# Attention and two MLP layers: weight conversions bound to later steps, flips of two pairs in other banks, norms and splits in another order

## The chip, the cores and the metric

The kernel runs on one core of a Trainium2 chip. The time is device time of one execution in microseconds (us), the median of several runs; lower is better.

## What is computed

```python
q_n, k_n = rmsnorm(q, g_q), rmsnorm(k, g_k)          # q, k, v: 4 x 12 heads x 448 x 64, f32
attn = softmax(q_n @ k_n.T / sqrt(64))               # per head, over 448 keys
x = (attn @ v)                                       # laid out as 1792 tokens x 768
h = x @ w_in;  x = (s * relu(h)**2 + b) @ w_out      # 768 -> 2048 -> 768, weights 64 bit
h = x @ w2_in; out = (h * cos(h)) @ w2_out           # 768 -> 2048 -> 768, weights 64 bit
```

## The kernel before

**Attention.** There are 24 pairs of heads (4 batches of 448 tokens, 6 pairs each). Pairs are numbered here by their index from 0; a pair has four steps s = 4i to 4i + 3, one for each chunk of 112 queries. `attention` is a generator whose loop emits one step per turn: scores of both heads (two matmuls into `sc` banks), their row maxima on VectorE (`top`), the Exp on ScalarE (`pr`, which also gives the row sums), and for the step two back `turn`: transposes of `pr` on TensorE into `tp` banks, copied out as `pT` by ScalarE for one head and by VectorE for the other. In step 1 and 2 of a pair the next pair's normalised q and k are transposed by `flip` (`pt_q`, `pt_k`) and copied out by `unflip` (`qT` on ScalarE, `kT` on VectorE). In steps 2 and 3 `mix` multiplies the previous pair's `pT` by v (`av`), `spread` transposes the reciprocals of the row sums (`rt`, copied to `xf`), and in step 0 of the pair after it `finish` multiplies the two on VectorE. Norms go ahead by two or three pairs: `squares`, `means`, `norms`, on GpSimd for most pairs and on VectorE for pair 0. `scores` of a step waits for the Exp of two steps before it.

**Splits.** All matmuls of the two layers work in two parts, high and low, and three products. `split` (called by `keep` at the end of a pair of the first two batches) makes them of x: `xh` on ScalarE (L96), `xl` on GpSimd (L97). `load_weight` makes them of the weights, in blocks of 128 x 384: a raw 64-bit block is loaded (queue SP), ScalarE converts its high and low words (`c` L392, `t` L393), VectorE joins them in three steps (L397 `t`, L398 `c`, L399 `t`), the result is stored for later use (L402), and `halves` makes `wh` on ScalarE (L359) and `wl` on GpSimd (L360). Two blocks make one weight tile; tiles wh and wl have three buffers each. The first blocks in order: two tiles of w_in (blocks 1 to 4), two of w_out (5 to 8), two of w_in (9 to 12), and so on.

**Stages.** The first nine pairs run alone (`ALONE = 9`). From step 40 on, units of the first layer are emitted between the steps of the remaining pairs: `unit_in` (18 matmuls `ph`, L422) and `unit_out` (6 matmuls `po`, L474), at a rate worked out from costs. The first group is two ph tiles and six po sums of batch 0, the next begins with two further w_in tiles.

**Banks.** `bank` gives a pair with index under 9 the two banks `mo` of pool `psm` for flips, spread and sums, which from step 40 on are also those of `ph` and `po`; later pairs take the two `tp` banks, which the transposes of `turn` use too.

**Order.** A scheduler places the instructions of each engine's queue by a model of their times, and pulls an instruction forward where it thinks the engine idle, except where the program fixes an order: `line` chains the instructions it is given on one engine (on ScalarE and VectorE while no more than 36 Exps have been emitted), `issue_after` puts one instruction behind another in the queue of the same engine without a wait. c and t of the first 16 blocks are put behind an Exp of `exps`, the list of the second Exp of each step: block number p (from 0) behind step GATE + 4p for p up to 7, then two steps apart. With GATE = 8 that is the first step of pairs 2 to 9. wh, wl, xh and xl are bound to nothing.

Of the kernel before, what the change touches and what calls it, by code (L numbers as in the profile page):

```python
# [10 lines left out]
F32 = mybir.dt.float32  # L11
# [4 lines left out]
ALU = mybir.AluOpType  # L16
# [17 lines left out]
def body(ctx, tc, q, k, v, g_q, g_k, w1_in, w1_out, s_in, b_in, w2_in, w2_out, out):  # L34
    nc = tc.nc
# [3 lines left out]
    P = 128  # L39
# [9 lines left out]
    NT = 2 * S // P  # L49
    SKEW = 2  # L50
    LAG_T = 2
    START, GATE = 4, 8
    ALONE = 9
    PAIR = 12.1
    LOOK = 8
# [55 lines left out]
    def attention(keep):  # L111
        att, ps = pools["att"], pools["ps"]
        pairs = [(b, hp) for b in range(B) for hp in range(NP)]
        st = [dict() for _ in pairs]
        tail = {}

        def line(engine, first, last=None):
            if engine in tail and (engine == "PE" or len(exps) <= NCH * ALONE):
# [38 lines left out]
        def norms(i):  # L157
            b, hp = pairs[i]
            m, tiny = st[i]["m"], nc.vector if i == 0 else nc.gpsimd
            ln = att.tile([CP, 16], F32, tag="ln", name=f"ln_{b}_{hp}")  # L160
            line("ACT", nc.scalar.activation(ln, m, AF.Ln))
            y = att.tile([CP, 16], F32, tag="y", name=f"y_{b}_{hp}")
            line("ACT", nc.scalar.activation(y, ln, AF.Exp, scale=-0.5))
            z = att.tile([CP, 16], F32, tag="z", name=f"z_{b}_{hp}")
            tiny.tensor_tensor(z, y, y, ALU.mult)
            tiny.tensor_tensor(z, z, m, ALU.mult)
            tiny.tensor_scalar(z, z, -0.5, 1.5, ALU.mult, ALU.add)
            tiny.tensor_tensor(y, y, z, ALU.mult)
            rs = y.rearrange("p (a h c) -> p a h c", a=2, h=2)
            if i == 0:  # L170
                st[i]["rs"] = y[:, 0:2 * NCH]
            for n, nm in enumerate("qk"):
                if i == 0 and n == 0:
                    continue
                (nc.vector if i == 0 else nc.gpsimd).tensor_tensor(
                    st[i]["n" + nm].rearrange("p c h d -> p h c d"), st[i][nm],
                    rs[:, n].unsqueeze(3).to_broadcast([CP, 2, NCH, D]), ALU.mult)

        def bank(i, name):
            if i < ALONE:  # L180
                return psm.tile([P, 512], F32, tag="mo", name=name, bufs=2)
            return ps.tile([P, 512], F32, tag="tp", name=name)

        def flip(i, nm):
            b, hp = pairs[i]
            pt = bank(i, f"pt_{nm}_{b}_{hp}")[:, :S]
            src = st[i]["q by chunk"] if i == 0 and nm == "q" else st[i]["n" + nm]
            mm = [nc.tensor.transpose(pt[:, c * CP:(c + 1) * CP], src[:, c, :, :].rearrange("p h d -> p (h d)"), ident[:CP, :CP]) for c in range(NCH)]
            line("PE", mm[0], mm[-1])
            st[i]["p" + nm] = pt  # L190
# [63 lines left out]
        def spread(i):  # L254
            b, hp = pairs[i]
            rt = bank(i, f"rt_{b}_{hp}")[:, :S]
            mm = [nc.tensor.transpose(rt[:, c * CP:(c + 1) * CP], st[i]["rb"][:, c, :, :].rearrange("p h d -> p (h d)"), ident[:CP, :CP]) for c in range(NCH)]
            line("PE", mm[0], mm[-1])
            x = st[i]["x"] = att.tile([P, S], F32, tag="xf", name=f"xf_{b}_{hp}", bufs=1)
            line("ACT", nc.scalar.copy(x, rt))  # L260

        def mix(i, part):
# [11 lines left out]
        def finish(i):  # L274
            b, hp = pairs[i]
            x = st[i]["x"]
            line("DVE", nc.vector.tensor_tensor(x, st[i]["pa"], x, ALU.mult))
            keep(b, hp, x)
            st[i].clear()
            finished["pairs"] += 1  # L280

        def emit(f, i, *a):
            if 0 <= i < len(pairs):
# [19 lines left out]
        for s in range(n + 5):  # L303
            i, r = divmod(s, NCH)
            old = i - 1 if 0 < i <= len(pairs) else None
            alone = old is not None and old < ALONE
            cost = 0.0
            if r == 1:
                emit(load, i, "v")
                emit(flip, i + 1, "q")  # L310
                cost += 0.46
            if r == 2:
                emit(flip, i + 1, "k")
                cost += 0.46
            if s < n:
                scores(s)
                cost += 0.93
            if r == 1:
                emit(unflip, i + 1, "q")
            if r == 2:  # L320
                emit(unflip, i + 1, "k")
            if r == 3 and old is not None and not alone:
                finish(old)
            if LAG_T <= s < n + LAG_T:
                turn(s - LAG_T)
                cost += 0.9
            if r == 0:
                if 0 <= i - 2 < ALONE:
                    finish(i - 2)
                emit(reciprocals, i - 1)  # L330
            if r == 2 and old is not None:
                if alone:
                    mix(old, range(2))
                else:
                    spread(old)
                    mix(old, range(NCH))
                cost += 3.86
            if r == 3 and alone:
                spread(old)
                mix(old, range(2, NCH))  # L340
            if i == 0 and r in (1, 2):
                for part in ((squares,), (means, norms))[r - 1]:
                    part(2)
            if r == 0 and i > 0:
                emit(norms, i + 2)
            if r == 2:
                emit(squares, i + 3)
            if r == 3:
                emit(means, i + 3)
                emit(load, i + 4, "qk")  # L350
            yield cost
# [3 lines left out]
    plain = {}  # L355
    count = {"g": 0, "raw": 0}

    def halves(w, wh, wl, eng=nc.gpsimd):
        nc.scalar.copy(wh, w)  # L359
        eng.tensor_tensor(wl, w, wh.bitcast(F32), ALU.subtract)  # L360

    def load_weight(key):
        layer, seg, kind, a, e = key
        w = ((w1_in, w1_out), (w2_in, w2_out))[layer][kind]
        name = "_".join(map(str, key))
        wh = wp.tile([P, 2 * CW], F32R, tag="wh", name=f"wh_{name}", bufs=3)
        wl = wp.tile([P, 2 * CW], F32R, tag="wl", name=f"wl_{name}", bufs=3)
        weights[key] = wh, wl
        for o in range(2):
            kk = f"{name}_{o}"  # L370
            hi_part, lo_part = (z[:, o * CW:(o + 1) * CW] for z in (wh, wl))
            if (layer, kind, a, e, o) in plain:
                t = wp.tile([P, CW], F32, tag="t", name=f"t_{kk}", bufs=3)
                nc.sync.dma_start(t, plain[layer, kind, a, e, o])
                halves(t, hi_part, lo_part, nc.vector)
                continue
            own = "xb" in pools or count["raw"] % 3 < 2
            raw = (wp if own else pools["att"]).tile([P, CW], I64, tag="raw", name=f"raw_{kk}", bufs=2 if own else 1)
            count["raw"] += 1
            if kind == 0:  # L380
                src = w[o * CW:(o + 1) * CW, a * P:(a + 1) * P].rearrange("(c p) f -> p c f", p=P)
                dma = nc.sync.dma_start(raw.rearrange("p (c f) -> p c f", f=P), src)
            else:
                dma = nc.sync.dma_start(raw, w[(CF * a + o) * P:(CF * a + o + 1) * P, e * CW:(e + 1) * CW])
            if seg == 0 and kind == 0 and a == 0:
                follow(dma, marks["start"])
            ru = raw.bitcast(U32).rearrange("p (n two) -> p n two", two=2)
            lo, hi = ru[:, :, 0], ru[:, :, 1]
            c = wp.tile([P, CW], U32, tag="c", name=f"c_{kk}", bufs=2)
            cf = c.bitcast(F32)  # L390
            t = wp.tile([P, CW], U32, tag="t", name=f"t_{kk}", bufs=3)
            for z in (nc.scalar.activation(cf, hi.bitcast(F32), AF.Copy, scale=2.0**-112),  # L392
                      nc.scalar.activation(t, lo, AF.Copy, scale=LSCALE, bias=-0.5)):  # L393
                p = count["raw"] - 1
                if p < 16:
                    issue_after(z, exps[min(GATE + 4 * min(p, 7) + 2 * max(p - 7, 0), len(exps) - 1)])
            nc.vector.scalar_tensor_tensor(t, hi, 0x80000000, t, ALU.bitwise_and, ALU.bitwise_or)  # L397
            nc.vector.tensor_scalar(cf, cf, VMAX, -VMAX, ALU.min, ALU.max)  # L398
            nc.vector.scalar_tensor_tensor(t, c, 3, t, ALU.logical_shift_left, ALU.bitwise_or)  # L399
            if layer == 0:  # L400
                d = dram.tile([P, CW], F32, tag=f"w_{kk}", name=f"wd_{kk}")
                nc.sync.dma_start(d, t.bitcast(F32))  # L402
                plain[layer, kind, a, e, o] = d
            halves(t.bitcast(F32), hi_part, lo_part)


    g = {}
# [264 lines left out]
```

## Time and profile before

| | us |
|---|---|
| median of 3 runs | 1315.2 (1314.98 to 1315.31) |
| the profiled execution | 1311.66 |
| its span, first to last instruction | 1309.9 |
| TensorE busy | 1251.1 (96%) |
| VectorE busy | 850.3 (65%) |
| ScalarE busy | 745.4 (57%) |
| GpSimd busy | 585.5 (45%) |

In the rows PE is TensorE's matmuls, PEld its weight loads, DVE VectorE, ACT ScalarE, POOL GpSimd; L228 is a line of the kernel; `tp<-ident,pr` names what is written and read. Clocks are TensorE's granted clock, 1.00 for 2.4 GHz and 0.50 for 1.2 GHz. Matmul ends are modelled, so that a busy TensorE is not one at its peak.

### The profile page before, as it was taken

How to read it: one execution, taken by the hardware profiler on the slowest of the kernel's cores; microseconds unless marked ns; L12 is line 12 of the kernel's file. 1: busy time of each engine (PE TensorE's matmuls, PEld its weight loads, DVE VectorE, ACT ScalarE, POOL GpSimd, SP SyncE). 2: the span in 40 equal slices, each digit the busy share in tenths (PEclk: the TensorE clock that was granted, in tenths of full speed). 3: DMA queues.
4: the chain of work that ended last, by engine and by line, in shares of the span. 5: the costliest groups of instructions: out<-in, count | busy, mean ns of one | idle time of the engine just before them, and what ended most of it. 6: DMA issues, size and time to landing. Idle time of an engine off the chain costs nothing.

```text
span 1309.9 us, 18652 instructions
## 1 busy us (share of the span) xinstructions
PE 1251.1 (96%) x6624; PEld 1036.7 (79%) x6624; DVE 850.3 (65%) x1456; ACT 745.4 (57%) x1674; POOL 585.5 (45%) x643
## 2 busy tenths in 40 slices
PE   5988998999999999999999999999999999999998
PEld 3444575677676666779999999989999999999997
DVE  6787666867777675664344545864767767666655
ACT  5676666756665555534432334788656657565641
POOL 4666454644545434234332233554544445354531
PEclk9999999999999999999999999999999999999999
DMA  4333332543434233254221212121212221111105
GB/s 120 94 90 93 93 107 75 164 136 102 137 101 131 94 90 114 82 177 125 78 81 49 61 55 73 41 69 49 61 36 73 60 62 49 49 49 49 49 14 169
DMA packets 82222, 111.33 MB, mean 85 GB/s; under 512 B 8112, under 2 KB 72144, under 8 KB 82128
## 3 DMA queue, kind: packets, MB, share of 16 engines
q1 hardware_dynamic: 82128, 110.13, 28.3%
q8 instruction: 52, 0.85, 0.3%
q14 instruction: 42, 0.34, 0.1%
HBM read 86.51 MB, written 23.59 MB: 84 GB/s over the span
## 4 chain that ended last, share of the span: by engine, by line
PE 64%; DVE 12%; ACT 11%; DMA 5%; POOL 3%; issue 3%; SPq 0%; ACTq 0%; DVEq 0%; POOLq 0%
PE ph L422 25%; PE po L501 15%; PE po L474 13%; PE av L269 4%; PE sc L208 4%; ACT pr L228 3%; PE tp L246 3%; DVE t L397 3%; DMA raw<-in_moe_w_in_dram 3%; DVE top L220 2%; ACT c L392 1%; DVE t L399 1%; DVE gt L447 1%; ACT pT L252 1%; DMA raw<-in_moe_w_out_dram 1%
## 5 line engine op out<-in xcount | busy, mean ns | idle before, releaser
L422 PE MATMUL ph<-xh,wl 128*128 128x448 f32 x768 | 283.5, 369 | 0.0
L422 PE MATMUL ph<-xh,wh 128*128 128x448 f32 x768 | 281.0, 371 | 1.6 <-ACT hs L440 1.6
L422 PE MATMUL ph<-xl,wh 128*128 128x448 f32 x768 | 282.4, 368 | 0.0
L452 POOL TENSOR_TENSOR gl<-gt,gh 128x448 fp32r<-128x448 f32 x128 | 157.7, 1237 | 180.0 <-ACT gh L451 179.9
L360 POOL TENSOR_TENSOR wl<-t,wh 128x384 fp32r<-128x384 f32 x128 | 139.0, 1103 | 91.7 <-ACT wh L359 85.6
L228 ACT ACTIVATE pr<-sc,top 112x448 f32<-112x448 f32 x184 | 116.2, 636 | 78.8 <-DVE top L220 78.4
L422 PEld LDWEIGHTS ph<-xh,wh 128*128 128x128 f32 x768 | 144.6, 188 | 19.5 <-issue 2.7
L501 PE MATMUL po<-wh,gh 128*128 128x384 f32 x448 | 151.9, 339 | 3.6 <-DVE acc L509 1.7
L474 PE MATMUL po<-gh,wh 128*128 128x448 f32 x384 | 145.7, 381 | 9.7 <-DVE acc L483 9.1
L422 PEld LDWEIGHTS ph<-xl,wh 128*128 128x128 f32 x768 | 144.7, 188 | 11.7 <-issue 1.3
L422 PEld LDWEIGHTS ph<-xh,wl 128*128 128x128 f32 x768 | 144.8, 188 | 11.3 <-issue 1.3
L483 DVE TENSOR_TENSOR acc<-po,acc 128x448 f32<-128x448 f32 x168 | 103.0, 618 | 77.7 <-PE po L474 77.5
L501 PE MATMUL po<-wh,gl 128*128 128x384 f32 x448 | 149.8, 334 | 0.0
L359 ACT CAST wh<-t 128x384 fp32r<-128x384 f32 x200 | 95.2, 512 | 95.7 <-PE po L474 52.3
L501 PE MATMUL po<-wl,gh 128*128 128x384 f32 x448 | 149.5, 334 | 0.0
L474 PE MATMUL po<-gh,wl 128*128 128x448 f32 x384 | 141.7, 369 | 0.0
L474 PE MATMUL po<-gl,wh 128*128 128x448 f32 x384 | 141.4, 369 | 0.0
L220 DVE TENSOR_REDUCE top<-sc 112x1 f32<-112x448 f32 x192 | 112.8, 616 | 38.1 <-PE sc L208 37.8
L509 DVE TENSOR_TENSOR acc<-po,acc 128x384 f32<-128x384 f32 x196 | 105.2, 550 | 48.4 <-PE po L501 48.4
L246 PEld LDWEIGHTS tp<-ident,pr 112*112 112x112 f32 x768 | 79.3, 134 | 71.6 <-issue 19.8
L450 POOL TENSOR_TENSOR gt<-hs,gt 128x448 f32<-128x448 f32 x64 | 78.6, 1228 | 118.9 <-ACT gt L449 108.7
L392 ACT ACTIVATE c<-raw 128x384 f32<-128x384 f32 x128 | 70.9, 554 | 103.7 <-DMA raw<-in_moe_w_in_dram 41.9
(89 smaller groups left out, 2261.0 us busy)
## 6 DMA issues: line engine op xcount, KB each, us to landing
raw<-in_moe_w_in_dram SPq DMA_DIRECT2D x64, 384.0 KB, 3.5
raw<-in_moe_w_out_dram SPq DMA_DIRECT2D x64, 384.0 KB, 3.2
t<-wd SPq DMA_DIRECT2D x72, 192.0 KB, 2.4
wd<-t SPq DMA_DIRECT2D x64, 192.0 KB, 3.4
rawk<-in_k_dram SPq DMA_DIRECT2D x24, 224.0 KB, 3.1
rawv<-in_v_dram SPq DMA_DIRECT2D x24, 224.0 KB, 3.4
rawq<-in_q_dram SPq DMA_DIRECT2D x23, 224.0 KB, 2.6
xd<-xf SPq DMA_DIRECT2D x12, 224.0 KB, 3.7
```

What stands on the lines that cost most here:

```text
L220: line("DVE", nc.vector.tensor_reduce(tops[j], sc[j], axis=AX.X, op=ALU.max, negate=True))
L228: e = line("ACT", nc.scalar.activation(pr, sc[j], AF.Exp, bias=tops[j], scale=scale[j], accum_out=st[i]["sums"][:, c, j:j + 1]))
L246: mm = [nc.tensor.transpose(tp[:, kc * CP:(kc + 1) * CP], pr[:, kc * CP:(kc + 1) * CP], ident[:CP, :CP]) for kc in range(NCH)]
L359: nc.scalar.copy(wh, w)
L360: eng.tensor_tensor(wl, w, wh.bitcast(F32), ALU.subtract)
L392: for z in (nc.scalar.activation(cf, hi.bitcast(F32), AF.Copy, scale=2.0**-112), nc.scalar.activation(t, lo, AF.Copy, scale=LSCALE, bias=- ...
L422: nc.tensor.matmul(h, a, m, start=(c == 0 and n == 0), stop=(c == NE - 1 and n == 2))
L452: nc.gpsimd.tensor_tensor(gl, gt, gh.bitcast(F32), ALU.subtract)
L474: marks["out"] = nc.tensor.matmul(po, a, m, start=(f == 0 and n == 0), stop=(f == CF - 1 and n == 2))
L483: nc.vector.tensor_tensor(at, po, at, ALU.add)
L501: nc.tensor.matmul(po, a, m, start=(f == 0 and n == 0), stop=(f == CF - 1 and n == 2))
L509: nc.vector.tensor_tensor(at, po, at, ALU.add)
```

## The change

c and t of every gated block are bound two steps later: behind the third step's Exp of pairs 2 to 9 for the first eight blocks, and two steps later for the others too. wh of the first eight blocks is bound behind the Exp of the step after that. The flips of pairs 9 and 10 take the `mo` banks. The vector steps of pair 0's norms are chained on VectorE in program order. For pairs 0 to 7 `keep` (xh, xl) is emitted in the fourth step after `mix` instead of in the first step, and `xf` has two buffers for it.

```diff
@@ -49,7 +49,7 @@
     NT = 2 * S // P
     SKEW = 2
     LAG_T = 2
-    START, GATE = 4, 8
+    START, GATE = 4, 10
     ALONE = 9
     PAIR = 12.1
     LOOK = 8
@@ -113,6 +113,7 @@
         pairs = [(b, hp) for b in range(B) for hp in range(NP)]
         st = [dict() for _ in pairs]
         tail = {}
+        held = []
 
         def line(engine, first, last=None):
             if engine in tail and (engine == "PE" or len(exps) <= NCH * ALONE):
@@ -162,19 +163,20 @@
             y = att.tile([CP, 16], F32, tag="y", name=f"y_{b}_{hp}")
             line("ACT", nc.scalar.activation(y, ln, AF.Exp, scale=-0.5))
             z = att.tile([CP, 16], F32, tag="z", name=f"z_{b}_{hp}")
-            tiny.tensor_tensor(z, y, y, ALU.mult)
-            tiny.tensor_tensor(z, z, m, ALU.mult)
-            tiny.tensor_scalar(z, z, -0.5, 1.5, ALU.mult, ALU.add)
-            tiny.tensor_tensor(y, y, z, ALU.mult)
+            kept = (lambda z: line("DVE", z)) if i == 0 else lambda z: z
+            kept(tiny.tensor_tensor(z, y, y, ALU.mult))
+            kept(tiny.tensor_tensor(z, z, m, ALU.mult))
+            kept(tiny.tensor_scalar(z, z, -0.5, 1.5, ALU.mult, ALU.add))
+            kept(tiny.tensor_tensor(y, y, z, ALU.mult))
             rs = y.rearrange("p (a h c) -> p a h c", a=2, h=2)
             if i == 0:
                 st[i]["rs"] = y[:, 0:2 * NCH]
             for n, nm in enumerate("qk"):
                 if i == 0 and n == 0:
                     continue
-                (nc.vector if i == 0 else nc.gpsimd).tensor_tensor(
+                kept(tiny.tensor_tensor(
                     st[i]["n" + nm].rearrange("p c h d -> p h c d"), st[i][nm],
-                    rs[:, n].unsqueeze(3).to_broadcast([CP, 2, NCH, D]), ALU.mult)
+                    rs[:, n].unsqueeze(3).to_broadcast([CP, 2, NCH, D]), ALU.mult))
 
         def bank(i, name):
             if i < ALONE:
@@ -183,7 +185,7 @@
 
         def flip(i, nm):
             b, hp = pairs[i]
-            pt = bank(i, f"pt_{nm}_{b}_{hp}")[:, :S]
+            pt = bank(i - 2, f"pt_{nm}_{b}_{hp}")[:, :S]
             src = st[i]["q by chunk"] if i == 0 and nm == "q" else st[i]["n" + nm]
             mm = [nc.tensor.transpose(pt[:, c * CP:(c + 1) * CP], src[:, c, :, :].rearrange("p h d -> p (h d)"), ident[:CP, :CP]) for c in range(NCH)]
             line("PE", mm[0], mm[-1])
@@ -256,7 +258,7 @@
             rt = bank(i, f"rt_{b}_{hp}")[:, :S]
             mm = [nc.tensor.transpose(rt[:, c * CP:(c + 1) * CP], st[i]["rb"][:, c, :, :].rearrange("p h d -> p (h d)"), ident[:CP, :CP]) for c in range(NCH)]
             line("PE", mm[0], mm[-1])
-            x = st[i]["x"] = att.tile([P, S], F32, tag="xf", name=f"xf_{b}_{hp}", bufs=1)
+            x = st[i]["x"] = att.tile([P, S], F32, tag="xf", name=f"xf_{b}_{hp}")
             line("ACT", nc.scalar.copy(x, rt))
 
         def mix(i, part):
@@ -275,9 +277,17 @@
             b, hp = pairs[i]
             x = st[i]["x"]
             line("DVE", nc.vector.tensor_tensor(x, st[i]["pa"], x, ALU.mult))
-            keep(b, hp, x)
             st[i].clear()
-            finished["pairs"] += 1
+            if i < ALONE - 1:
+                held.append((b, hp, x))
+            else:
+                keep(b, hp, x)
+                finished["pairs"] += 1
+
+        def settle():
+            while held:
+                keep(*held.pop(0))
+                finished["pairs"] += 1
 
         def emit(f, i, *a):
             if 0 <= i < len(pairs):
@@ -338,6 +348,8 @@
             if r == 3 and alone:
                 spread(old)
                 mix(old, range(2, NCH))
+            if r == 3 and 0 <= i - 2 < ALONE:
+                settle()
             if i == 0 and r in (1, 2):
                 for part in ((squares,), (means, norms))[r - 1]:
                     part(2)
@@ -355,8 +367,10 @@
     plain = {}
     count = {"g": 0, "raw": 0}
 
-    def halves(w, wh, wl, eng=nc.gpsimd):
-        nc.scalar.copy(wh, w)
+    def halves(w, wh, wl, eng=nc.gpsimd, behind=None):
+        z = nc.scalar.copy(wh, w)
+        if behind is not None:
+            issue_after(z, behind)
         eng.tensor_tensor(wl, w, wh.bitcast(F32), ALU.subtract)
 
     def load_weight(key):
@@ -389,11 +403,12 @@
             c = wp.tile([P, CW], U32, tag="c", name=f"c_{kk}", bufs=2)
             cf = c.bitcast(F32)
             t = wp.tile([P, CW], U32, tag="t", name=f"t_{kk}", bufs=3)
+            gate = GATE + 4 * min(count["raw"] - 1, 7) + 2 * max(count["raw"] - 8, 0)
+            gate = min(gate, len(exps) - 1) if count["raw"] <= 16 else None
             for z in (nc.scalar.activation(cf, hi.bitcast(F32), AF.Copy, scale=2.0**-112),
                       nc.scalar.activation(t, lo, AF.Copy, scale=LSCALE, bias=-0.5)):
-                p = count["raw"] - 1
-                if p < 16:
-                    issue_after(z, exps[min(GATE + 4 * min(p, 7) + 2 * max(p - 7, 0), len(exps) - 1)])
+                if gate is not None:
+                    issue_after(z, exps[gate])
             nc.vector.scalar_tensor_tensor(t, hi, 0x80000000, t, ALU.bitwise_and, ALU.bitwise_or)
             nc.vector.tensor_scalar(cf, cf, VMAX, -VMAX, ALU.min, ALU.max)
             nc.vector.scalar_tensor_tensor(t, c, 3, t, ALU.logical_shift_left, ALU.bitwise_or)
@@ -401,7 +416,7 @@
                 d = dram.tile([P, CW], F32, tag=f"w_{kk}", name=f"wd_{kk}")
                 nc.sync.dma_start(d, t.bitcast(F32))
                 plain[layer, kind, a, e, o] = d
-            halves(t.bitcast(F32), hi_part, lo_part)
+            halves(t.bitcast(F32), hi_part, lo_part, behind=exps[gate + 1] if count["raw"] <= 8 and gate + 1 < len(exps) else None)
 
 
     g = {}
```

## Rows read from the trace of the kernel before

**Rows 1.** Windows: two pairs' stretches, index 9's and the rest; busy us per engine, TensorE clock
```profile
core 0: us, PE busy (x) PEld busy (x) DVE busy (x) ACT busy (x) POOL busy (x), PEclk, DMA share, GB/s
37.87:51.14 13.27, 12.15 (x80) 6.29 (x78) 10.71 (x21) 9.71 (x29) 8.47 (x13) 1.00 0.28 82
...
117.41:139.50 22.09, 16.45 (x79) 7.97 (x77) 11.96 (x22) 9.60 (x28) 8.11 (x12) 0.77 0.23 67
139.50:154.39 14.89, 12.53 (x78) 6.28 (x76) 12.51 (x24) 12.03 (x34) 8.35 (x16) 1.00 0.33 97
154.39:1309.90 1155.51, 1124.74 (x5894) 972.71 (x5892) 738.17 (x1246) 644.76 (x1392) 500.80 (x501) 1.00 0.28 83
```

**Rows 2.** Chain that ended last, one regular pair (index 4): start us, us, what
```profile
67.96 0.45 ACT c L392
68.41 0.46 ACT t L393
68.87 0.45 ACT xh L96
...
69.44 1.23 ACT pr L228 x4
...
71.58 0.60 PE tp L246 x4
```

**Rows 3.** Timeline of TensorE, pairs 1 and 4: third and fourth scores (start us, us)
```profile
30.30 1.01 PE L208 MATMUL sc<-kT,qT 64*112 64x448 f32 x4
...
33.98 1.01 PE L208 MATMUL sc<-kT,qT 64*112 64x448 f32 x4
...
68.85 1.01 PE L208 MATMUL sc<-kT,qT 64*112 64x448 f32 x4
...
73.76 1.01 PE L208 MATMUL sc<-kT,qT 64*112 64x448 f32 x4
```

**Rows 4.** Timeline of pair 4; in brackets the idle time before, with its releaser
```profile
67.67 0.61 DVE L220 TENSOR_REDUCE top<-sc 112x1 f32<-112x448 f32 x1
...
75.46 0.63 ACT L228 ACTIVATE pr<-sc,top 112x448 f32<-112x448 f32 x1 [1.86 <-DVE top L220]
...
79.35 0.63 ACT L228 ACTIVATE pr<-sc,top 112x448 f32<-112x448 f32 x1 [1.69 <-DVE top L220]
```

**Rows 5.** VectorE's conversion lines, 36 to 125 us: ns min/median/max, first to last start
```profile
L398 DVE TENSOR_SCALAR c<-c x7: 359/361/789, 41.9 to 121.5; 128x384 f32<-128x384 f32 x7
...
L397 DVE SCALAR_TENSOR_TENSOR t<-raw,t x7: 548/548/1523, 42.7 to 122.7; 128x384 uint32<-128x384 uint32 x7
...
L399 DVE SCALAR_TENSOR_TENSOR t<-c,t x7: 543/969/976, 43.7 to 124.7; 128x384 uint32<-128x384 uint32 x7
```

**Rows 6.** Timeline of the ninth pair (index 8): GpSimd and TensorE
```profile
122.69 1.13 POOL L97 TENSOR_TENSOR xl<-xf,xh 128x448 fp32r<-128x448 f32 x1
...
126.00 1.00 PE L246 MATMUL tp<-ident,pr 112*112 112x112 f32 x4 [3.68 <-ACT qT L197]
```

**Rows 7.** Windows: the stretch behind that wait
```profile
126.00:134.00 8.00, 7.00 (x26) 3.76 (x28) 3.00 (x5) 2.15 (x6) 3.47 (x5) 0.50 0.39 122
```

**Rows 8.** Timeline of TensorE in the tenth pair (index 9)
```profile
146.09 0.57 PE L188 MATMUL pt_k<-ident,nk 112*128 112x112 f32 x4 [1.17 <-ACT pT L252]
```

**Rows 9.** Timeline of the opening
```profile
9.20 0.68 DVE L152 TENSOR_REDUCE ss<-nk 112x8 f32<-112x512 f32 x1
...
11.33 1.04 POOL L144 TENSOR_TENSOR nq<-rawq 112x512 f32<-112x512 f32 x1 [0.79 <-DMA rawq<-in_q_dram]
```

**Rows 10.** Timeline around the thirteenth weight block, three engines
```profile
189.78 0.55 ACT L392 ACTIVATE c<-raw 128x384 f32<-128x384 f32 x1
...
193.71 0.36 PE L422 MATMUL ph<-xh,wh 128*128 128x448 f32 x1
...
193.98 1.01 POOL L360 TENSOR_TENSOR wl<-t,wh 128x384 fp32r<-128x384 f32 x1 [1.04 <-ACT wh L359]
```

**Rows 11.** Windows: a stretch with attention and the first layer mixed
```profile
242.00:246.00 4.00, 1.40 (x9) 0.98 (x8) 4.00 (x9) 3.67 (x10) 2.52 (x4) 0.87 0.23 69
```

**Rows 12.** What TensorE waited for, 154 to 1310 us: total us, times, longest
```profile
PE po L474 <- ACT wh L359: 0.4, 1, 0.4
```

## Prediction, made before the changed kernel was run

> **What bounds the kernel now.** I read the page's table of 40 slices first: TensorE is busy in nearly every slice from the sixth on, but the first four or five have gaps. The windows by pair of heads then split the run in two [rows 1]. From 154.39 us to the end TensorE is busy 1124.74 of 1155.51 us, so that part is TensorE's own work and moves only if it starts sooner or if its few gaps change. Before it, nine pairs run alone with two more being prepared: a pair in the regular stretch takes 13.27 us with TensorE busy 12.15 (no gap of its own is long, but the matrices are small), the ninth takes 22.09 us and the tenth 14.89. These are what the change can reach.
>
> Next the chain of waits in one regular pair [rows 2]. After the Exp of the first step of a pair, ScalarE runs the two conversions c and t of a weight block and the copy xh of a finished x, 0.45, 0.46 and 0.45 us, and only then the Exp of the second step at 69.44; the transposes that need ScalarE's copies start at 71.58. All three stand on the chain; nothing else late is to be seen there. The same distance without them is in the trace: in the second pair (index 1), where no conversion and no xh runs yet, third to fourth scores matmul is 30.30 to 33.98, 3.68 us; in a regular pair it is 68.85 to 73.76, 4.91 us [rows 3].
>
> **The change part by part.**
> *Conversions and high parts, regular pairs.* The gate moves c and t from behind the first step's Exp to behind the third's. ScalarE idles 1.86 us before the fourth step's Exp [rows 4], and c plus t need 0.91: covered. The block's high part wh, now bound behind the fourth step's Exp, goes into the 1.69 us before the next pair's first Exp, again covered. The xh of a pair is written three steps later in the program; since it is bound to nothing, it may or may not leave its place. What is then late? The Exp of the second step needs its row maximum, whose first half ends at 67.67 + 0.61 = 68.28 [rows 4], so that Exp can start at about 68.33 and not before: 1.11 us sooner than 69.44. If xh stays, only 0.91 goes. The other comparison, 4.91 against 3.68, gives 1.23 as the most. I take 1.05, near the limit set by the row maximum: a regular pair takes 13.27 - 1.05 = 12.22. Six pairs (index 2 to 7): **6.3 us**, ends 5.5 and 7.4.
>
> *What moves along.* Each c and t is followed by three VectorE steps, L398, L397 and L399, medians 0.36, 0.55 and 0.97 us, longest 0.79, 1.52 and 0.98 [rows 5]. They now fall between the third and the fourth step's row maxima. VectorE is busy 10.71 of 13.27 us [rows 1]; at 12.22 it still has 1.5 us free, so at the median they fit, and a delay of the fourth step's maximum by up to about 1 us is taken up by ScalarE's idle 1.69 us behind it. The store of the block and the next raw load, issued by SyncE behind them, move about 5 us later in a round of 12 to 13; nobody waits for them within that time. GpSimd's xl and wl move with xh and wh; their readers are matmuls of the stage after 154.39. The longest values come from GpSimd: L397 took 1.52 us at 122.7, while GpSimd's xl ran 1.13 us from 122.69 [rows 5, 6], and ended 0.4 us after it. The Trainium skill, page "SBUF — State Buffer", section "Who interferes with whom", says that VectorE steps with two SBUF inputs share a port with GpSimd's reads and that the second to start waits until the first is done. The trace agrees with that, 1.52 against 0.55 us. By that rule, taken in full, the three steps would wait beside the norms' GpSimd work, and the sum would be that of the first rival, 1305.8 us.
>
> *Flips of the pairs with index 9 and 10.* In the ninth pair's window the next pair's flips take the two transposes' banks. The transposes then wait for the copy out of a flip: TensorE stands 3.68 us until qT [rows 6], and in the stretch behind that wait its granted clock is 0.50, the 1.2 GHz level [rows 7]. With the flips in the sums' two banks this pair runs as the eight before it do, which share those banks among flips, spread and sums without such a wait: 22.09 - 12.22 = **9.9 us**. If only the regular 13.27 is reached: 8.8. The tenth pair's two waits for a flip's bank (the longer 1.17 us [rows 8]) go as well; it has two Square steps on ScalarE that earlier pairs don't have, so I take 12.4 instead of 12.22: 14.89 - 12.4 = **2.5 us**, ends 1.6 and 2.7.
>
> *First norms in order.* Two sums of squares of pair 1, 0.68 us each [rows 9], no longer stand before pair 0's scaling on VectorE, so its first scores can come 1.36 us sooner. But pair 1's flip needs GpSimd's norm, and GpSimd is held by a square whose input lands at about 11.3 us [rows 9], not by VectorE. I take **0**; the ends are 0.5 us lost (pair 1's means come later) and 1.3 gained.
>
> *The weights that follow.* The blocks from the ninth on are also gated two Exps later. Two steps later the twelfth block stands where the thirteenth stands now: converted from 189.78, its low part done at 193.98 + 1.01 = 194.99. TensorE reaches the matmul that wants the twelfth (second half of the second tile in the group after the first sums) at 193.71 [rows 10], so it would come 1.3 us late there. The other end is the jam at 242 to 246 us: VectorE busy 4.00 of 4.00, TensorE 1.40, granted clock 0.87 [rows 11], 2.6 us of idle and 0.5 of slow clock: 3.1 lost if one more such jam comes, 2 gained if most of this one goes. I take **1.0 lost**, by the row of the twelfth block, since attention's transposes can fill a part of it.
>
> **Sum.** 6.3 + 9.9 + 2.5 + 0 - 1.0 = 17.7 us off the profiled execution's 1311.66 us (span 1309.9 and 1.8 around it): 1294.0. The median of the runs shown is 1315.2, 3.5 us above the profiled one; the same saving gives **1297.5 us**. With all ends it is 1292 to 1303.
>
> **The rivals.**
> 1. *VectorE's conversion steps become the late ones* (0.17). Against GpSimd's norms they cost up to 0.79 + 1.52 + 0.98 = 3.29 instead of 1.88 us [rows 5]; VectorE then needs 10.71 + 1.41 = 12.1 of 12.22 us, and standing in its queue ahead of the fourth row maximum they hold the Exp. For it: L399's median is already its longest. Against it: about 1 us of delay is absorbed. If pairs stay at 13.27, 8.8 + 1.6 - 1.0 = 9.4 us are won: 1305.8; partly so, 1301 to 1306.
> 2. *Late weights, slower* (0.10, of which 0.03 slower). The later gates of blocks nine to sixteen leave TensorE waiting for a weight after 154.39, long enough that its clock falls as it did after the 3.68 us gap. One such event costs what the ninth pair shows, 22.09 - 13.27 = 8.8 us: 1315.2 - 18.7 + 8.8 = 1305.3. It makes the kernel slower from 18.7 us on, that is with a third event: 1315.2 - 18.7 + 26.4 = 1322.9. Against it: behind 154.39 us the list of TensorE's waits has one for a weight's part, 0.4 us [rows 12].
> 3. *The flips don't come free* (0.05): a sum held in those banks until its pair is finished makes the flip wait, and the ninth pair keeps its gap. Then six regular pairs give 6.3, the ninth's own Exp 1.0, the weights -1.0: 6.3, so 1308.9. Against it: the eight pairs before use the same banks so.
> 4. *More than that* (0.06): the opening gives its 1.3 us and the jam after 210 us eases: about 1291.
>
> **How the numbers follow.** The forecast has 0.62. The range 1291.5 to 1306 takes in the forecast, nearly all of rival 1, the one-event form of rival 2 and half of rival 4, and leaves out the rest, under 2 in 10. A measurement of this kernel tells about 0.2%, 2.6 us, from no change. Only rival 2's worst form is slower (0.03); 0.03 more is for mixtures of rivals 2 and 3 that end within 0.2%; 0.94 is faster.
>
> **What would show it.** Right: windows of about 12.2 us for pairs 2 to 8, the stage that now begins at 154.39 beginning at about 136, no granted clock below 1.00 between pair 2 and there, c and t ahead of the fourth step's Exp and wh behind it. Wrong: L397 to L399 ending after the fourth scores matmul and regular pairs still over 13 us; a TensorE wait at a flip in the ninth pair; or that stage beginning at 136 with the end less than 15 us sooner, which would put the loss into the stage of rival 2.

## The result and the profile after

The changed kernel takes **1300.75 us** (median of 4 runs, 1299.74 to 1302.61) against 1315.26 for the kernel before: a ratio of 0.989, interval 0.9873 to 0.9907, or 14.5 us. The forecast was 1297.5, that is 17.7 us less: the direction was right and 3.2 us of the gain were missing.

Of the two profiled executions, before's (1311.66 us) lies 3.6 us below its median and after's (1302.61 us, span 1300.8) 1.9 above. Profile against profile shows only 9.1 us. The medians are therefore used for the end, and the traces for the stages ahead of it.

The windows of the kernel after, cut at the first scores matmul of a pair as [rows 1] are; same columns. The first is pair 2, the next the ninth pair (index 8), then the tenth and the rest:

```profile
40.29:52.65 12.36, 12.08 (x79) 6.29 (x77) 10.17 (x20) 8.64 (x27) 6.76 (x11) 1.00 0.21 53
114.40:126.76 12.36, 12.08 (x80) 6.29 (x78) 11.04 (x21) 9.88 (x29) 7.96 (x13) 1.00 0.35 107
126.76:139.08 12.32, 11.98 (x79) 6.27 (x77) 10.93 (x22) 10.59 (x31) 7.05 (x16) 1.00 0.38 110
139.08:1300.80 1161.72, 1129.27 (x5894) 976.07 (x5892) 747.02 (x1249) 647.07 (x1396) 506.95 (x503) 0.99 0.28 84
```

Every pair from pair 2 on now takes 12.3 to 12.4 us, the ninth (22.09 before) and the tenth (14.89) included, and no clock below 1.00 is left there. Pair 2 starts at 40.29 instead of 37.87 [rows 1], though: before anything was won, 2.4 us were lost. The stage behind starts at 139.08 instead of 154.39, 15.3 us sooner.

The waits of TensorE in the kernel after, 38 to 139 us (total us, times, longest): one kind is all that is listed, and the 3.68 us wait for qT [rows 6] is gone.

```profile
PE tp L248 <- ACT pT L254: 2.3, 8, 0.3
```

The chain of waits through one regular pair of the kernel after (start us, us, what), the counterpart of [rows 2]:

```profile
66.69 1.34 ACT pr L230 x4
68.03 0.42 ACT pT L254
68.46 0.12 ACT ln L162
68.57 0.46 ACT xh L96
69.03 0.11 ACT y L164
69.14 1.23 ACT pr L230 x4
```

c and t are gone from it. xh still stands between the first and the second step's Exp: it was written three steps later in the program, but nothing binds it, and the scheduler left it where it was.

The conversions in the same pair, on the timeline of the kernel after (start us, us; in brackets the idle time before):

```profile
72.81 0.57 ACT L408 ACTIVATE c<-raw 128x384 f32<-128x384 f32 x1
73.27 0.55 ACT L409 ACTIVATE t<-raw 128x384 uint32<-128x384 uint32 x1
73.28 1.04 POOL L177 TENSOR_TENSOR nk<-rawk,y 112x512 f32<-112x512 f32 x1
73.41 1.13 DVE L413 TENSOR_SCALAR c<-c 128x384 f32<-128x384 f32 x1 [0.63 <-ACT c L408]
74.46 0.55 DVE L412 SCALAR_TENSOR_TENSOR t<-raw,t 128x384 uint32<-128x384 uint32 x1
75.47 0.54 DVE L414 SCALAR_TENSOR_TENSOR t<-c,t 128x384 uint32<-128x384 uint32 x1
75.58 0.63 ACT L230 ACTIVATE pr<-sc,top 112x448 f32<-112x448 f32 x1 [1.76 <-DVE top L222]
```

They lie in ScalarE's wait for the fourth step, as forecast. The clip (L398 before, L413 now) takes 1.13 us where it took 0.36 [rows 5]. It stands in VectorE's queue ahead of the fourth step's row maximum, whose end the Exp waits for (the 1.76 us). But the list of TensorE's waits above has none for an Exp, so nothing shows that this costs a pair time.

The opening, GpSimd's and TensorE's steps of pairs 1 and 2 on the timeline of the kernel after, the counterpart of [rows 9]:

```profile
11.28 1.04 POOL L145 TENSOR_TENSOR nq<-rawq 112x512 f32<-112x512 f32 x1 [9.97 <-DMA rawq<-in_q_dram]
12.40 0.20 POOL L156 TENSOR_SCALAR m<-ss 112x16 f32<-112x16 f32 x1
...
14.19 1.04 POOL L145 TENSOR_TENSOR nk<-rawk 112x512 f32<-112x512 f32 x1 [1.59 <-DMA rawk<-in_k_dram]
15.19 0.21 POOL L167 TENSOR_TENSOR z<-y 112x16 f32<-112x16 f32 x1
...
17.47 1.01 PE L190 MATMUL pt_q<-ident,nq 112*128 112x112 f32 x4 [4.58 <-POOL nq L177]
```

Here the 2.4 us went. In the kernel before the same steps ran as follows (timeline of the kernel before):

```profile
9.96 0.57 POOL L155 TENSOR_SCALAR m<-ss 112x16 f32<-112x16 f32 x1 [8.66 <-DVE ss L152]
...
12.33 0.21 POOL L165 TENSOR_TENSOR z<-y 112x16 f32<-112x16 f32 x1
...
14.61 1.01 PE L188 MATMUL pt_q<-ident,nq 112*128 112x112 f32 x4 [0.30 <-POOL nq L175]
15.51 1.05 POOL L144 TENSOR_TENSOR nk<-rawk 112x512 f32<-112x512 f32 x1
```

Pair 1's small GpSimd steps (m, then z and what follows it) used to run ahead of pair 2's second square. After the change both squares of pair 2 stand ahead of z, and the second waits 1.59 us for its input. Pair 1's first flip starts 2.86 us later.

### The profile page after: what moved, and what is told of

Same layout as the page of the kernel before. It is cut to its first block, busy times and chain, and to the rows that moved or that the text cites. A ratio compares the mean times of both kernels' runs of the same rounds, so it can differ in the third digit from the quotient of the medians.

```text
span 1300.8 us, 18641 instructions
## 1 busy us (share of the span) xinstructions
PE 1249.6 (96%) x6624; PEld 1038.3 (80%) x6624; DVE 857.8 (66%) x1456; ACT 746.1 (57%) x1674; POOL 585.6 (45%) x643
## 4 chain that ended last, share of the span: by engine, by line
PE 62%; DVE 13%; ACT 12%; POOL 5%; DMA 4%; issue 4%; SPq 0%; DVEq 0%; ACTq 0%; POOLq 0%
PE ph L437 25%; PE po L516 15%; PE po L489 13%; ACT pr L230 3%; PE av L271 3%; PE sc L210 3%; DVE t L412 3%; DMA raw<-in_moe_w_in_dram 2%; PE tp L248 2%; DVE top L222 2%; DVE t L414 2%; POOL wl L374 1%; ACT pT L254 1%; DVE gt L462 1%; DVE gt L452 1%
```

## The experiments

The table gives the start of the scores matmul of step 8 (pair 2) and of step 40 (the stage behind), and the Exp of step 56, all in us from the traces; then the median of the runs and the ratio to the kernel before on the same chip.

| kernel | step 8 | step 40 | Exp 56 | us | ratio, interval |
|---|---|---|---|---|---|
| before | 37.87 | 154.39 | 258.62 | 1315.26 | |
| after | 40.29 | 139.08 | 245.50 | 1300.75 | 0.9890 (0.9873 to 0.9907) |
| after, again | 40.91 | 139.76 | 244.60 | 1301.64 | 0.9896 (0.9868 to 0.9925) |
| no chain of norms | 37.33 | 136.16 | 242.83 | 1298.26 | 0.9872 (0.9841 to 0.9902) |
| old gates from the ninth block | 40.72 | 139.54 | 244.69 | 1299.82 | 0.9886 (0.9854 to 0.9919) |
| xh bound | 41.11 | 139.46 | 244.06 | 1299.51 | 0.9880 (0.9854 to 0.9907) |
| flips alone | 37.25 | 143.82 | 246.76 | 1306.50 | 0.9945 (0.9924 to 0.9966) |
| gates alone | 37.85 | 143.27 | 250.44 | 1305.72 | 0.9937 (0.9915 to 0.9960) |
| xh, xl written early | 40.07 | 138.90 | 244.84 | 1299.84 | 0.9902 (0.9874 to 0.9930) |
| GpSimd's order fixed | 36.43 | 135.27 | 241.75 | 1297.29 | 0.9873 (0.9848 to 0.9898) |
| chain of norms alone | 39.52 | 156.02 | 261.85 | 1315.58 | 1.0016 (0.9994 to 1.0039) |
| order fixed, xh bound | 36.66 | 135.01 | 239.95 | 1298.45 | 0.9887 (0.9847 to 0.9928) |

The ratios belong to medians of the kernel before of 1315.26 for the kernel after, 1314.67 for the next four rows, 1313.36 for flips, gates, xh and xl early and GpSimd's order, and 1313.26 for the last two; what a variant gains in the text is against these. Executions of one kernel differ by several us (the kernel before from 1309.04 to 1324.41 over these comparisons), so differences of 1 to 3 us between variants are read at steps 8 and 40 and not from the medians. There the two traces of the changed kernel agree within 0.7 us; over the five kernels with the same opening as it, step 8 lies between 40.07 and 41.11.

**The change again.** The kernel is the changed one.

> The changed kernel beside the kernel before, to hold the next three against. Expected: 1300 to 1302 us, some 14 us under the kernel before; regular pairs 12.35 us from scores to scores, the tenth pair's end (scores of step 40) at about 139.2 us, the first flip of pair 1 at about 17.5 us. If the 7 us that the profiled run lost again behind 190 us belong to the kernel, the profile shows them again; if they are chance of one run, it doesn't.

Measured: 1301.64 us, pairs of 12.36 us, pair 1's first flip at 17.52, step 8 at 40.91 and step 40 at 139.76. The loss in the opening and the new period both repeat. The loss behind step 40 repeats in part only: of a lead of 14.6 us over before's profiled execution 2.9 are gone at the end of the span, where the first profiled execution lost 6.2 of 15.3.

**The chain of the first norms taken out.** Everything else of the change stays.

```diff
-            kept(tiny.tensor_tensor(z, y, y, ALU.mult))
+            tiny.tensor_tensor(z, y, y, ALU.mult)
```

(and so for the other four steps under `kept`)

> The changed kernel without the VectorE chain of pair 0's norms; everything else of the change stays. Theory: that chain delays pair 1's means by 2 us and GpSimd then takes two squares of pair 2, one of them waiting for a load, ahead of pair 1's norm, so pair 1's first flip comes at 17.5 instead of 14.6 us. Without the chain the flip is back at 14.6 us, step 40 begins 2.4 us sooner (136.8), and the time is 2 to 3 us under the changed kernel's. Rival: the late flip comes from slower loads in that run; then the flip stays near 17.5 us or moves without a change of GpSimd's order, and the time stays.

Measured: pair 1's first flip at 14.44, step 40 at 136.16, 2.9 and 3.6 us sooner than in the changed kernel's two executions (2.4 expected), and 1298.26 against 1301.64 us in the medians, whose intervals overlap. The timeline of this kernel's opening has the old order on GpSimd back, m ahead of the first square and z right behind it:

```profile
10.02 0.57 POOL L156 TENSOR_SCALAR m<-ss 112x16 f32<-112x16 f32 x1 [8.71 <-DVE ss L153]
...
11.16 1.04 POOL L145 TENSOR_TENSOR nq<-rawq 112x512 f32<-112x512 f32 x1 [0.57 <-ACT y L164]
12.16 0.21 POOL L166 TENSOR_TENSOR z<-y 112x16 f32<-112x16 f32 x1
```

The chain that orders VectorE is what turned GpSimd's order round.

**The old gates from the ninth block on.** The gates of blocks nine to sixteen go back to where they were before the change.

```diff
+            gate -= 2 * (count["raw"] > 8)
```

> The changed kernel with the gates of weight blocks 9 to 16 as before (two Exps sooner than in the change). Theory: the later gates push conversions into the stage at 190 to 245 us, where VectorE is full, and cost about 4 us there; with the old gates the lead over the kernel before stays at 16 to 17 us from step 96's Exp on, and the time is 2 to 4 us under the changed kernel's. Rival: the loss there comes from the jam itself, which takes in any sooner start; then the lead falls from 17 to 13 us there as it does in the changed kernel, and the time is within 1 us of it.

Measured: the Exp of step 40 comes 1.5 us later than in the changed kernel (144.83 against 143.36), its scores matmul 0.2 us sooner, and step 56 is level, 244.69 against 244.60. The later Exp costs TensorE nothing: in the changed kernel's own window from the scores to the Exp of step 40 it is busy 3.59 of 3.59 us, with matmuls of the first layer.

```profile
139.08:142.67 3.59, 3.59 (x23) 2.80 (x22) 1.55 (x5) 1.53 (x5) 2.82 (x4) 1.00 0.71 216
```

The 2 to 4 us that the theory expected are not shown: the lead over the kernel before falls here too, to 13.3 us at the Exp of step 92 (11.4 in the changed kernel's second execution), and the medians, 1299.82 and 1301.64, lie 1.8 us apart with intervals that overlap. Neither a gain nor a loss of these later gates is shown, nor the 1.0 us that I had put down for them.

**xh bound to a step.** xh of pairs 0 to 7 is put behind the last Exp that is written when it is.

```diff
-                keep(*held.pop(0))
+                keep(*held.pop(0), exps[-1])
-        nc.scalar.copy(hi, src)
+        z = nc.scalar.copy(hi, src)
+        if behind is not None:
+            issue_after(z, behind)
```

> The changed kernel with xh of pairs 0 to 7 bound behind the Exp of the step in which it is emitted (the fourth), so that it can't stand before the second step's Exp. Theory: xh is the last thing on the chain that can go; the Exp of the second step is then held by its row maximum, 0.2 us sooner: a regular pair takes 12.15 us instead of 12.35, eight pairs give 1.4 to 1.6 us. Rival: xh stood in a wait anyway (the row maximum is the later one already): 12.35 us stays and the time is the same.

Measured, one pair's window:

```profile
65.61:77.86 12.25, 12.07 (x79) 6.28 (x77) 10.50 (x21) 10.15 (x29) 7.92 (x13) 1.00 0.34 106
```

xh leaves the chain (it now starts at 65.46, ahead of the first step's Exp) and the period falls by 0.11 us, not by its 0.46 and less than the 0.2 expected. On the chain of this pair the second step's Exp now stands behind its row maximum:

```profile
68.97 0.54 DVE top L224
69.52 0.03 issue
69.54 1.34 ACT pr L232 x4
```

The row maxima come next, as the prediction's limit from [rows 4] had it: their share of the chain between 60 and 80 us is 14.1% here against 6.2% in the kernel after. TensorE is busy 12.07 of the 12.25 us, so little is left to win in a pair. Over the pairs the gain is under 1 us, and the median doesn't resolve it.

**The flips' banks alone**, in the kernel before.

```diff
-            pt = bank(i, f"pt_{nm}_{b}_{hp}")[:, :S]
+            pt = bank(i - 2, f"pt_{nm}_{b}_{hp}")[:, :S]
```

> The kernel before with one part of the change: the flips of pairs 9 and 10 in the sums' two banks. Theory: the gap of 3.7 us in the ninth pair and the clock of 0.50 behind it come from the two transposes' banks being held by flips; with the banks changed alone that pair takes the regular 13.3 us instead of 22.1 and the tenth 13.3 instead of 14.9, so step 40 begins 10.4 us sooner, at 144.0 us, and the time falls by 7 to 10.5 us. Rival: the gap comes from the weight conversion in VectorE's queue (0.79 and 1.52 us ahead of the row maxima); then the ninth pair still has a TensorE wait of over 2 us and takes 17 us or more.

Measured, the windows of the ninth and the tenth pair (a regular one takes 13.27 as before):

```profile
116.83:130.09 13.26, 12.14 (x79) 6.28 (x77) 10.69 (x22) 9.40 (x28) 7.54 (x12) 1.00 0.37 111
130.09:143.82 13.73, 12.13 (x79) 6.28 (x77) 12.55 (x24) 11.43 (x33) 7.14 (x15) 1.00 0.30 95
```

The ninth pair becomes a regular one, 8.8 us off, and step 40 comes 10.6 us sooner (0.6 of it already at step 8); the time falls by 6.9 us, just under the 7 to 10.5 expected. The rival, that the conversions in VectorE's queue made the gap and not the banks, falls: the conversions stand here where they stood before, and the gap is gone.

**The gates alone**, in the kernel before: GATE 10, and wh behind the following step. Of the rest only the second buffer of `xf` stayed in.

```diff
-    START, GATE = 4, 8
+    START, GATE = 4, 10
-            halves(t.bitcast(F32), hi_part, lo_part)
+            halves(t.bitcast(F32), hi_part, lo_part, behind=exps[gate + 1] if count["raw"] <= 8 and gate + 1 < len(exps) else None)
```

> The kernel before with one part of the change: the gates of c, t and wh. Theory: regular pairs fall from 13.27 to 12.35 us, six pairs give 5.5 us; the ninth pair keeps its banks and so a gap, the tenth its two waits; the time falls by 4 to 7 us. Rival: the conversion was what made the gap of the ninth pair, and moving it removes the gap too; then the ninth pair takes under 15 us and the time falls by over 12 us.

Measured, the windows of the ninth and the tenth pair (a regular one takes 12.36), then TensorE's wait for qT in these pairs:

```profile
111.99:128.89 16.90, 12.57 (x79) 6.28 (x77) 11.61 (x23) 10.75 (x30) 8.14 (x14) 1.00 0.36 111
128.89:143.27 14.38, 12.23 (x78) 6.29 (x77) 10.73 (x20) 10.10 (x29) 8.23 (x16) 1.00 0.18 52
```

```profile
PE tp L246 <- ACT qT L197: 2.0, 1, 2.0
```

The 12.36 us of a regular pair come with the gates of c, t and wh (the second `xf` buffer has no part in it, see the next run). They also take 5.2 us off the ninth pair without its banks: the wait for qT is 2.0 us instead of 3.68, and behind it the clock stays at 1.00 where it was 0.50 [rows 7]. 3.9 of the 5.2 us are TensorE's busy time, 12.57 instead of 16.45 for the same 79 matmuls [rows 1]. The pair lies between the theory and its rival (under 15 us), and the time falls by 7.6 us, a little more than the 4 to 7 expected. So the gap needs the flips' banks, the conversions lengthen it, and the gains of the two parts overlap in that pair. Alone they win 10.6 and 11.1 us at step 40, together, without the chain of norms, 18.2.

**xh and xl written early again**: the later place in the program taken back.

```diff
-            if i < ALONE - 1:
-                held.append((b, hp, x))
-            else:
-                keep(b, hp, x)
-                finished["pairs"] += 1
+            keep(b, hp, x)
+            finished["pairs"] += 1
```

> The changed kernel without the later emission of xh and xl and without the second xf buffer. Theory: xh is bound to nothing and stands in the same place, between the first and the second step's Exp, whenever it is emitted; regular pairs stay at 12.35 us and the time within 1 us of the changed kernel's. Rival: the later emission or the second buffer is what let the pairs run at 12.35; then they are slower, by up to 0.45 us each.

Measured: pairs of 12.36 us, and 1299.84 us. Writing xh later does nothing here that can be measured. The edit leaves the second buffer of `xf` in, other than the expectation says, and no run has the new gates without it. But the trace of this run shows that it isn't needed in a regular pair: the copy into `xf` at 77.81 comes 7.8 us after xl, the last reader of the pair before it, has ended (68.90 + 1.13 = 70.03); in the gates alone it is 75.58 after 67.81.

**GpSimd's order fixed.** The chain of norms stays, and pair 2's squares are bound behind pair 1's last norm.

```diff
+                if i == 1:
+                    marks["norm"] = z
...
+                    if i == 2:
+                        issue_after(z, marks["norm"])
```

> The changed kernel with the VectorE chain of pair 0's norms kept, and GpSimd's two squares of pair 2 put behind pair 1's norm in its queue. Theory: GpSimd's order, not the chain itself, makes the opening late; with it mended the chain's earlier scores come through: pair 1's first flip at about 13.2 us, 1.4 sooner than in the kernel before and 4.3 sooner than in the changed one, step 40 begins 3 to 4 us sooner than in the changed kernel, and the time is 3 to 4 us under it. Rival: pair 2's norm, now later, becomes the late one; then step 40 gains 2.5 us or less.

Measured: step 40 at 135.27, 3.8 and 4.5 us ahead of the changed kernel's two executions (3 to 4 expected) and 0.9 ahead of the kernel without the chain. The timeline of its opening:

```profile
12.80 1.04 POOL L179 TENSOR_TENSOR nq<-rawq,y 112x512 f32<-112x512 f32 x1
...
13.90 1.01 PE L194 MATMUL pt_q<-ident,nq 112*128 112x112 f32 x4 [0.58 <-POOL nq L179]
```

Pair 1's flip came at 17.47 after the change; here it comes at 13.90, behind nq and ahead of pair 2's first square (14.80), sooner than in the kernel before (14.61). The 0.9 us are what the chain is worth with its side effect removed, unless the new order gives a part of them by itself: that order without the chain was not run. The median of 1297.29 us is the lowest of all, but its interval overlaps the changed kernel's.

**The chain of norms alone**, in the kernel before.

```diff
+            kept = (lambda z: line("DVE", z)) if i == 0 else lambda z: z
+            kept(tiny.tensor_tensor(z, y, y, ALU.mult))
```

(and so for the other steps)

> The kernel before with one part of the change: the VectorE chain of pair 0's norms. Theory: alone it makes pair 1's first flip 2.5 to 3 us late, as in the changed kernel (17.3 to 17.9 us against 14.6), the third pair's first scores 2.4 to 3 us late, pairs and the ninth pair's gap stay as in the kernel before, and the time is 0 to 4 us over it. Rival: the lateness is there only together with the other parts; then the third pair's first Exp stays at 39.6 us.

Measured: the opening with the two steps that matter turned round as in the changed kernel,

```profile
13.01 1.04 POOL L144 TENSOR_TENSOR nk<-rawk 112x512 f32<-112x512 f32 x1 [0.67 <-DMA rawk<-in_k_dram]
14.00 0.22 POOL L166 TENSOR_TENSOR z<-y 112x16 f32<-112x16 f32 x1
```

pair 1's first flip at 16.29 (17.3 to 17.9 expected) and step 8 at 39.52, 1.65 us late (2.4 to 3 expected). The third pair's first Exp comes at 41.22 instead of 39.57, so the rival falls. The wait for the input is 0.67 us here and 1.59 in the changed kernel, so part of the size hangs on when that load lands. The time, 2.3 us more, can't be told from no change (0.9994 to 1.0039).

**GpSimd's order fixed and xh bound**, the two repairs together.

> The changed kernel with both mends: GpSimd's squares of pair 2 behind pair 1's norm, and xh bound behind the fourth step's Exp. Theory: the two add up, 4.4 us in the opening and 0.11 us for each of eight pairs; step 40's Exp at about 138.0 us instead of 142.7 or 143.4, and of these 5 us about 2 to 4 reach the end: 1296 to 1299 us. Rival: xh in its later place delays GpSimd's norms of the next pairs once the opening is sooner; then regular pairs are 12.36 us or longer and the time is not under that of the kernel with the opening alone mended.

Measured: pairs of 12.25 us, step 40 at 135.01, Exp 56 the earliest of all at 239.95. The two add up at step 40 to 0.26 us more than the first repair alone, which no median here resolves; the tenth pair, which takes 12.60 us (12.32 in the changed kernel), gives a part of it back. The rival's mechanism isn't seen either, since the pairs stay at 12.25. The time of 1298.45 us (0.9847 to 0.9928) is not better than with the first repair alone.

## Why the prediction was right, and where it was not

**What bounds the kernel, and the ninth pair: right.** 9.9 us were forecast and 9.73 measured (22.09 to 12.36); the lower end for the regular period alone, 8.8, is just what the flips' banks gave by themselves (13.26). The tenth pair gave 2.57 for 2.5. One thing was not seen: with the gates alone the same pair loses 5.2 us of its length. With the flips in the sums' banks there is no gap, but while they shared the transposes' banks its length hung on the conversions too.

**Regular pairs: right in kind, a little too large.** 0.91 us each instead of 1.05, 5.4 instead of 6.3 over six. The step named the reason, "if xh stays, only 0.91 goes", and then took the other end. The limit from the row maximum, 12.22, was good: with xh bound a pair takes 12.25. Of the signs named for being right, the order came (c and t ahead of the fourth step's Exp, wh behind it, at 77.61 in the pair shown above), and so did the clock of 1.00. The windows are 12.36 instead of about 12.2, and the next stage starts at 139.08 instead of about 136, most of which is the opening's.

**Opening: the term that was mis-sized.** Forecast 0, with 0.5 us lost as the worst end; measured 2.4 lost in the profiled execution and 3.0 in the second (steps 8), and 2.9 and 3.6 against the same two at step 40 by taking the chain out. The first half was right: pair 0's scaling of nk on VectorE came sooner, 8.37 instead of 9.79, with pair 1's two sums of squares now behind it (the second is shown). VectorE in the kernel after,

```profile
8.37 0.69 DVE L177 TENSOR_TENSOR nk<-rawk,y 112x512 f32<-112x512 f32 x1
9.64 0.68 DVE L153 TENSOR_REDUCE ss<-nk 112x8 f32<-112x512 f32 x1
```

and in the kernel before:

```profile
9.79 0.68 DVE L175 TENSOR_TENSOR nk<-rawk,y 112x512 f32<-112x512 f32 x1
```

What failed is the sentence that GpSimd is held by a square whose input lands at about 11.3 us [rows 9], as if its order stood. That order is not written out: m and z are bound to nothing, and the scheduler places them by its model of the times. With pair 1's sums of squares later on VectorE it put the squares first. On the chip that was the wrong way round: the sums end at 9.64 + 0.68 = 10.32 us, so m could have run ahead of the square at 11.28, and it stands behind it in the queue, as z stands behind the second. I priced the delay of m as a delay, not as a change of place behind two loads.

**VectorE's conversion steps (rival 1): half true, without the price.** The clip does wait beside GpSimd's scaling:

```profile
L413 DVE TENSOR_SCALAR c<-c x6: 1114/1126/1133, 48.7 to 110.5; 128x384 f32<-128x384 f32 x6
```

(One line of VectorE between 36 and 120 us of the kernel after; ns min, median, max.) Its median rose from 361 to 1126 ns, but L399's 969 became 543 as L414 (0.54 in the timeline above), so the three steps need 2.21 us against 1.88 at the medians before. No wait of TensorE for an Exp came of it. In the pair shown the clip started 0.13 us after GpSimd's step and ended 0.22 after it; in all six blocks it started 0.12 to 0.15 us after that step. The Trainium skill, "SBUF — State Buffer", section "Who interferes with whom", says that such a scalar step on VectorE, where it runs in its two-port mode, can be locked out by GpSimd for a whole instruction, and that the order of issue decides; these rows agree.

**The flips don't come free (rival 3): false.** No wait of TensorE for a flip's bank or for its copy is left in pairs 2 to 9.

**More than that (rival 4): false.** Its price does not follow from its own terms either: the opening's 1.3 and the weights' 2 gained in place of 1.0 lost make 1293.2, not about 1291.

**Weights (the 1.0 lost, and rival 2).** No late weight stops TensorE: behind 139.08 us its list of waits has one for a weight's high part, 0.4 us as before [rows 12].

```profile
PE po L489 <- ACT wh L371: 0.4, 1, 0.4
```

The old gates put back make no difference at step 56. The 1.0 us is not shown as what I took it for.

**The sum.** At step 40 the terms add up: 5.4 + 9.7 + 2.6 - 2.4 = 15.3 us, which is 154.39 - 139.08. Of 18.7 forecast there, 2.4 were lost in the opening and 0.9 in the regular pairs. From there to the end the medians keep 14.5 and the profiled pair 9.1. That the 0.8 us between 15.3 and 14.5 come near the 1.0 put down for the weights is luck, since no late weight stands behind them.

**What lies behind step 40, partly open.** Two executions of the same changed kernel, and the flips alone, show the same jam of VectorE that [rows 11] shows for before. The kernel after:

```profile
228.00:232.00 4.00, 1.90 (x9) 1.33 (x10) 4.00 (x9) 2.96 (x8) 2.01 (x3) 0.66 0.16 29
232.00:236.00 4.00, 4.00 (x12) 3.51 (x11) 4.00 (x7) 2.43 (x7) 3.83 (x5) 0.50 0.83 230
```

TensorE stands 2.1 us in the first of these windows (and 1.2 in the four us ahead of it), and the clock goes to 0.50. In the flips alone it stands 2.6 us, from 229 to 237 us, and the clock stays at 1.00. The jam came forward with everything else and did not ease.

That the profiled pair keeps 6.2 us less at the end than at step 40 is not shown to be this jam, though. In the twelve profiled executions TensorE is idle 30.2 to 32.5 us behind step 40, nearly the same, while its 5894 matmuls there take 1124.1 to 1134.3 us. Of the 6.2 us, 4.5 are such busy time (1129.27 against 1124.74). And the chain of norms alone, which leaves that stage as it was before, has there

```profile
156.02:1317.00 1160.98, 1129.26 (x5894) 975.31 (x5892) 739.78 (x1246) 645.11 (x1392) 499.89 (x501) 0.99 0.28 83
```

against 1155.51 and 1124.74 for before [rows 1]: 5.5 us more without a change of the stage. So the 6.2 us lie within what executions differ by, and before's profiled one was a short one. In the medians most variants keep up to 4.6 us less than they lead by at step 40 (the flips alone 10.6 and 6.9, the gates alone 11.1 and 7.6, the order fixed 19.1 and 16.1; the old gates 14.9 and 14.9). These leads are taken from one execution of the kernel before; whether a stage behind step 40 takes a part of them back was not separated.

## What to carry to other kernels

Where one engine's steps are put in an order by hand and another's are not, the second order can turn round: name the steps there that nothing binds, read from the trace which of them wait for loads, and price a change of place as well as a delay. A step that is to leave a busy spot must be bound to its new one, since writing it later in the program may leave it where it was. And a gain ahead of a stage that is bound elsewhere is to be measured by medians at the end as well as by the trace at the stage's start.

## What was not expected of the hardware

A wait of TensorE did not always cost clock. Behind 3.68 us the granted clock was 0.50 [rows 7], behind the 2.0 us of the gates alone it stayed at 1.00. Even one kernel differs from execution to execution. The window between the Exps of steps 52 and 56 is in the kernel after

```profile
207.78:245.50 37.72, 32.65 (x158) 23.83 (x157) 32.57 (x55) 27.36 (x67) 27.46 (x26) 0.86 0.58 176
```

and in its second profiled execution

```profile
208.39:244.60 36.21, 31.03 (x158) 22.59 (x157) 32.42 (x55) 27.53 (x66) 27.19 (x26) 0.91 0.59 182
```

The same 158 matmuls take 1.6 us more at the lower clock, and the idle time is the same, 5.1 and 5.2 us. That is as much as one of the smaller terms of the sum, and over all of the time behind step 40 the matmuls' busy time differs by up to 10 us between the twelve executions, their idle time by 2.3. So two profiles alone could not settle the small terms.
